# Chunk attention feeding a wave MLP: middle chunks' scores on four row tiles of TensorE, and another order of the whole program with q, k, v of the second group and q, k of the third loaded ahead of the token weights

## The chip, the cores and the metric

The kernel runs on one core of a Trainium2 chip. The core has five engines that each work through their own list of instructions: TensorE (PE in the profile; PEld is its weight load), VectorE (DVE), ScalarE (ACT), GpSimd (POOL) and SyncE (SP). DMAs are issued by POOL, SP and ACT and are carried by 16 DMA engines that all issuers share. The metric is the device time of one launch in microseconds; the median of the runs is what counts.

## The reference

Inputs are q, k, v of shape (8, 8, 576, 64) (batch, heads, sequence, head size) and four weight matrices. Attention works inside chunks of 64 positions:

```python
scores = scale * np.matmul(q_c, k_c.transpose(0, 1, 2, 4, 3))   # 9 chunks of 64 positions
scores = scores - np.max(scores, axis=-1, keepdims=True)
attn = np.exp(scores)
attn = attn / (np.sum(attn, axis=-1, keepdims=True) + 1e-09)
out = np.matmul(attn, v_c)
...
theta = x @ w_theta                                  # x: (8, 576, 512)
zr, zi = x * np.cos(theta), x * np.sin(theta)
y = np.einsum('ts,bsd->btd', w_tok_r, zr) + np.einsum('ts,bsd->btd', w_tok_i, zi)
u = x + y
return u + np.maximum(u @ w_ch, 0.0)
```

x is the attention output with the heads side by side. Everything is given and returned in float32; the kernel computes in float16 with float32 sums.

## The kernel before

**Tiles.** The batch is done in four pairs, p = 0 to 3. A pair's two sequences of 576 rows are nine tiles of 128 rows, j = 0 to 8: tiles 0 to 3 are the first four 128-row blocks of the first sequence, 4 to 7 those of the second, and tile 8 holds the last 64 rows of both, the "middle chunks". Attention goes by groups: A and B (tiles 0, 1 and 2, 3), C and D (4, 5 and 6, 7), each with four chunks of 64 positions, and M (tile 8) with two chunks, one of each sequence.

**Steps.** The program is a list of steps written out in one string, ORDER. A step "kind.where.slot" issues its instructions on its engines at that place; where is pair and group ("0M", "1A") or pair and tile ("37" is tile 7 of pair 3); the slot is a buffer or a PSUM bank (0 to 7). No scheduler moves anything afterwards, so each engine works in the order of the string. The kinds:

- qk, v: POOL issues the loads of a group's q and k (lines 158 to 175), or v (202 to 213), which cast to float16 on the way. q and k of an M group are four small DMAs, of any other group two; v is two or three. lw: token weights (242 to 247), lc: w_ch. hq, hk, lt: SP loads q, k of group 0A and w_theta as float32; cqa, ckv, cta cast them on ACT or DVE (196, 198, 262), ctv does it for w_theta on DVE.
- T (or Tq, Tk, Tk0, Tk1 for parts): DVE transposes q and k in 32x32 blocks (317).
- S (S0, S1: half of the heads): scores on PE (335), each product a 32-row by 64-column tile of the array. E: exponentials on ACT (361). V0, V1: times v on PE (378), N0, N1: division by the sum on DVE (393, 395).
- X: PE transposes x (415), xa and xv copy it to SBUF on ACT or DVE (440, 438); xd does both by one DMA transpose on SP's queue (432). H: theta on PE (453), G: cosine and sine on ACT (472), Z: x times them on DVE (488 to 495).
- TW: PE transposes a block of token weights (284), twv and twa copy it. Y (or Ya, Yb, Ym: parts of one sum): the token mix on PE (518), 18 products of 128x512 summed in one bank, or nine per half; A adds x on DVE (530).
- U with ua or uv: PE transposes u (535) and ACT or DVE copies it (547, 545); ud does it by a DMA transpose on SP's queue (543). W: times w_ch on PE (558), R: ReLU and sum on DVE (570); st, sa, sg: the store, issued by SP, ACT or POOL.
- dm.n.b: n products of a tile of zeros into bank b (154), which nothing reads.

**What sets the order of transfers.** POOL's loads go out in the order of the string, on eight semaphores in turn: a load isn't issued before the one eight places earlier has landed. In ORDER the first loads of POOL are q and k of 0M (four DMAs), v of 0M (two), v of 0A (three), token weights of block 2 (two), q and k of 0B (two), token weights 1 (two), v of 0B (three), token weights 0, q and k of 0C, token weights 3, and so on.

**Scores of an M group.** An M group has two chunks of 64 positions. Its q and k rows lie on partitions 0 to 63, a sequence on 32 of them (two positions in each), with all eight heads side by side, and after the transposes each product contracts over 32 partitions, twice (e = 0, 1). In the other groups the four chunks lie on the four quarters of 32 partitions, so that four row tiles of the array take turns; in an M group there are two. The innermost loop over c in lines 333 and 334 is this choice:

```python
for c in range(2 * n):                                  # n is 1 for an M group, else 2
    r, cc = (c // 2, c % 2) if n == 2 else (0, c)
    nc.tensor.matmul(ps[half[r ^ cc], r, h - hs[0]], ...)
```

r is the PSUM bank, half[...] the 64 partitions of it that are written.

Of the kernel before, what the change touches and what calls it, by code (L numbers as in the profile page):

```python
# [24 lines left out]
H0.0B.7 H1.0B.0 Tq.0C.0 G0.0B.2 G1.0B Tk.0C S.0C.3 twv.00 Ya.00.7 Z0.0B TW.03.5 Z1.0B Z.0M Yb.02  # L25
Ym.02 E.0C.3 Yb.00 Ym.00 A.02 Yb.01 Tq.0D.1 V1.0C.3 twa.03 A.00 V0.0C.0 Ym.01 Ya.03.5 Tk.0D
N1.0C S.0D.6 U.02.3 N0.0C ua.02.0 qk.1B.3 Yb.03 v.1M lw.04.2 X.0C.4 A.01 U.01.0 Ym.03 qk.1C.1
U.00.1 v.1B E.0D.0 A.03 V1.0D.2 N1.0D ua.01.1 qk.1D.4 qk.2M.12 v.1D V0.0D.6 xa.0C.3 v.2D qk.2C.5
v.1C W.02.0 N0.0D H.0C.4 U.03.2 ua.00.2 G.0C.0 T.1A.2 W.00.3 R.00.0 X.0D.1 S.1A.6 xv.0D.0 E.1A.1
v.2B qk.2A.6 W.01.3 H.0D.4 v.2M V0.1A.6 R.02.1 V1.1A.0 R.01.2 Ym.07.3 uv.03.3 G.0D.2 Ym.06.2  # L30
Z.0C N1.1A Ya.07 Ym.04.0 Ya.04 Ya.06 N0.1A W.03.1 X.1A.6 xa.1A.1 Z.0D Yb.06 T.1M.0 Yb.04 TW.04.4
R.03.3 twa.04 T.1B.1 S.1M.7 st.02 E.1M.2 A.04 A.06 S.1B.0 Yb.07 H.1A.4 V1.1M.6 qk.3M.7 qk.2B.8
v.2A A.07 N1.1M E.1B.3 V1.1B.2 st.01 V0.1B.0 N0.1B Y.08.7 V0.1M.6 N1.1B G.1A.1 U.06.0 ua.06.4
Ym.05.1 N0.1M X.1B.4 st.00 U.04.5 Ya.05 U.07.2 X.1M.3 xa.1B.2 A.08 T.1D.2 xv.1M.3 ua.04.5 H.1B.6
H.1M.0 v.3A qk.3A.9 ua.07.6 W.07.4 qk.3B.10 T.1C.0 G.1B.0 v.2C S.1C.2 S.1D.5 U.08.7 Yb.05 Z.1A
Z.1B G.1M.2 Z.1M uv.08.7 R.07.4 Y.12.0 E.1D.0 Y.11.7 v.3M A.12 E.1C.1 A.05 qk.3C.11 V0.1D.4
T.2M.1 V1.1D.2 V0.1C.0 Y.13.6 N1.1D W.08.2 N0.1D U.12.3 N0.1C A.11 X.1D.4 R.08.5 st.03 uv.12.0
T.2A.0 Y.10.5 A.10 A.13 V1.1C.0 S.2M.7 v.3C qk.2D.0 S.2A.2 N1.1C U.11.5 st.07 uv.11.2 W.06.6
st.08 X.1C.0 W.04.1 xa.1D.0 H.1D.4 E.2A.3 E.2M.2 R.04.1 R.06.3 U.05.2 xa.1C.1 T.2B.2 G.1D.1
H.1C.0 uv.05.1 T.2C.1 W.05.3 Z.1D st.04 R.05.2 S.2B.4 V1.2M.7 G.1C.0 Z.1C V0.2M.2 E.2B.0 sa.05  # L40
N1.2M W.11.6 U.10.0 ua.10.3 Y.17.1 N0.2M R.11.0 A.17 Y.15.7 V0.2B.4 V0.2A.2 A.15 N0.2B N0.2A
V1.2B.0 Y.18.6 A.18 S.2C.4 sa.11 X.2M.7 xv.2M.2 W.10.2 N1.2B R.10.4 E.2C.1 T.3M.0 H.2M.3 Y.16.6
U.13.7 G.2M.2 X.2B.4 V1.2A.0 A.16 st.06 st.10 uv.13.6 xa.2B.3 V0.2C.2 V1.2C.5 N1.2A N1.2C N0.2C
W.13.7 R.13.5 sa.13 X.2A.4 xd.2C.0 xv.2A.1 H.2B.0 U.18.5 U.17.6 U.16.2 uv.16.7 U.15.3 Y.14.7
ua.18.4 T.2D.2 Z.2M ua.17.5 ua.15.1 W.16.4 H.2A.5 G.2B.1 S.3M.2 S.2D.0 Z.2B G.2A.0 W.12.3 E.3M.2
R.16.1 A.14 Z.2A U.14.4 W.18.7 R.12.2 R.18.0 Y.21.5 Y.23.6 E.2D.0 st.18 V0.2D.2 T.3C.1 A.21
ua.14.2 v.3B T.3A.0 V1.2D.0 qk.3D.3 N1.2D N0.2D T.3B.2 sa.12 S.3A.4 W.14.7 sa.16 A.23 xd.2D.2
H.2C.0 E.3A.3 R.14.3 Y.22.4 G.2C.2 V0.3M.5 V1.3M.2 T.3D.0 A.22 Z.2C N1.3M st.14 S.3B.6 E.3B.1
S.3C.0 H.2D.3 E.3C.0 N0.3M W.15.6 Y.20.7 v.3D G.2D.1 ud.23.3 R.15.4 V0.3B.0 V0.3A.5 V1.3A.2 Z.2D
A.20 W.17.4 R.17.5 N0.3B Y.24.7 Y.27.4 N1.3A N0.3A A.27 V1.3B.0 xd.3M.3 N1.3B st.15 A.24 V1.3C.2  # L50
N1.3C S.3D.5 Y.28.4 H.3M.7 V0.3C.0 ud.20.6 E.3D.2 V0.3D.5 V1.3D.2 A.28 N0.3C N0.3D N1.3D xd.3A.1
G.3M.0 ud.27.7 W.27.4 Y.25.0 xd.3B.0 H.3A.5 A.25 ud.22.0 Y.26.1 G.3A.2 H.3B.2 ud.21.4 st.17 A.26
R.27.0 xd.3C.2 G.3B.1 H.3C.5 Z.3A W.21.7 xd.3D.3 Z.3M ud.24.2 G.3C.2 Z.3B R.21.2 Z.3C H.3D.0
# [11 lines left out]
def kernel(  # L65
# [11 lines left out]
    nc = tc.nc  # L77
# [226 lines left out]

    heads = {None: range(H), 0: range(H // 2), 1: range(H // 2, H)}

    def qk_t(which, f=None):

        def turn(p, g, slot=None):
            n = 64 if g == "M" else P  # L310
            if slot is not None:
                st["T", p, g] = buffer([P, 2, H, 32, 2, 2], "T", slot)
            a, z = {"q": (0, 1), "k": (1, 2), "qk": (0, 2)}[which]
            hs = slice(heads[f][0], heads[f][-1] + 1)
            src = st["qk", p, g][0:n, a:z, hs].rearrange("p w h s d -> p (w h s d)")
            to = st["T", p, g][0:n, a:z, hs].rearrange("p w h l s e -> p (w h l s e)")
            nc.vector.transpose(  # L317
                to.bitcast(FP32).rearrange("p (x l s) -> p x s l", l=32, s=2),
                src.bitcast(FP32).rearrange("p (x s d) -> p x s d", s=2, d=32),
            )  # L320

        return turn

    def scores(f):
        def products(p, g, b):
            n = size(g)
            hs = heads[f]
            ps = banks(b, n).rearrange("p (r x) -> p r x", r=n)[:, :, 0 : len(hs) * CH]
            ps = ps.rearrange("p r (h i) -> p r h i", i=CH)
            t = st["T", p, g].rearrange("p w h l s e -> p w h (l s) e")  # L330
            for h in hs:
                for e in range(2):
                    for c in range(2 * n):
                        r, cc = (c // 2, c % 2) if n == 2 else (0, c)
                        nc.tensor.matmul(  # L335
                            ps[half[r ^ cc], r, h - hs[0]],
                            t[quarter[c], 1, h, :, e],
                            t[quarter[c], 0, h, :, e],
                            start=(e == 0),
                            stop=(e == 1),  # L340
                            tile_position=(32 * c, CH * (r ^ cc)),
                        )
# [313 lines left out]
```

## Time and profile before

| | |
|---|---|
| runs | 194.37, 192.99, 193.19 us, median 193.19 |
| profiled execution | 194.09 us, its span 192.3 us |
| instructions in the profile | 6066, of them 2630 products on PE |

The span runs from the first to the last instruction of the core in the profile; 1.8 us of the profiled execution lie around it. All times below that are positions ("at 26.00") are microseconds from the start of the span. A line of a view in order of time gives start, length, engine, source line, operation and tile, how often, and in square brackets how long the engine had been idle and what ended that. A line of groups gives busy time, the mean of one instruction in nanoseconds, and the idle time ahead of them. The chain of waits follows the work that ended last back from the end, each piece with its start and length.

### The profile page before, as it was taken

What the parts mean: (1) busy time and instruction counts of PE and PEld (TensorE: products, weight loads), DVE (VectorE), ACT (ScalarE), POOL (GpSimd) and SP (SyncE); (2) the same over time, 40 slices, a digit from 0 to 9 for tenths busy, and PEclk for the clock granted to TensorE, in tenths of its full rate; (3) what the DMA queues carried; (4) which work ended last, traced back from release to release, by engine and by line L of the source; (5) the groups of instructions that cost most, each with busy time, mean ns of one, the idle gap of its engine ahead of it and who ended that gap; (6) DMA issues with size and microseconds to landing.
All of it is one profiled execution on the core that took longest, in us unless ns stands there. A gap on an engine that the chain in (4) does not pass through costs nothing.

```text
span 192.3 us, 6066 instructions
## 1 busy us (share of the span) xinstructions
PE 180.6 (94%) x2630; PEld 93.8 (49%) x2630; DVE 137.0 (71%) x254; ACT 101.2 (53%) x130; POOL 88.2 (46%) x125
## 2 busy tenths in 40 slices
PE   7569989999999999999999999999999999999980
PEld 2136445555464654555456554464544444444440
DVE  0155878967976988969788998967782963672761
ACT  3218797499759792289444665897164650000010
POOL 7788789579756996969388400000000000020400
PEclk9966999999999999999999999999999999999999
DMA  5999999999999999999999996542479217366693
GB/s 150 253 223 188 178 179 176 188 135 174 205 217 175 132 161 201 145 189 240 207 188 190 170 153 170 31 118 75 81 116 189 84 55 138 56 248 161 180 283 113
DMA packets 99002, 31.34 MB, mean 163 GB/s; under 512 B 90336, under 2 KB 94304, under 8 KB 98976
## 3 DMA queue, kind: packets, MB, share of 16 engines
q0 software_dynamic: 75568, 16.80, 95.2%
q1 hardware_dynamic: 21600, 11.01, 25.4%
q10 hardware_dynamic: 1808, 3.15, 4.5%
q8 instruction: 20, 0.33, 0.7%
q14 instruction: 6, 0.05, 0.1%
HBM read 33.06 MB, written 9.44 MB: 221 GB/s over the span
## 4 chain that ended last, share of the span: by engine, by line
PE 80%; DMA 6%; ACT 6%; DVE 3%; issue 1%; POOL 1%; DVEq 0%; POOLq 0%
PE psum L518 34%; PE psum L453 15%; PE psum L558 14%; PE psum L335 6%; DMA land<-in_k_dram 4%; PE psum L378 4%; DMA uT<-x 3%; PE psum L415 2%; PE psum L535 2%; ACT L140 2%; PE psum L154 2%; ACT cos L472 1%; ACT eT L361 1%; ACT sin L472 1%; PE psum L284 1%
## 5 line engine op out<-in xcount | busy, mean ns | idle before, releaser
L518 PEld LDWEIGHTS <-wT 128*128 128x128 f16 (+1 forms) x360 | 31.0, 100 | 34.5 <-issue 1.2
L210 POOL DMA_DIRECT2D v<-in_v_dram x56 | 41.9, 773 | 7.8 <-DMA land<-in_k_dram 2.7
L518 PE MATMUL psum<-zr,wT 128*128 128x512 f16 (+1 forms) x180 | 44.7, 380 | 0.0
L518 PE MATMUL psum<-zi,wT 128*128 128x512 f16 (+1 forms) x180 | 42.9, 379 | 0.0
L530 DVE TENSOR_TENSOR x<-psum,x 128x512 f16<-128x512 f32 x36 | 24.3, 685 | 19.4 <-PE psum L518 19.0
L558 PE MATMUL psum<-wch,uT 128*128 128x512 f16 (+1 forms) x148 | 35.4, 374 | 0.8 <-DMA uT<-x 0.8
L453 PE MATMUL psum<-wtheta,xT 128*128 128x512 f16 x144 | 34.2, 379 | 0.3 <-DVE xT L438 0.3
L586 POOL DMA_DIRECT2D out_dram<-o x4 | 2.2, 556 | 70.0 <-DVE o L570 70.0
L570 DVE SCALAR_TENSOR_TENSOR o<-psum,x 128x512 f32<-128x512 f32 (+1 forms) x37 | 24.0, 670 | 9.8 <-PE psum L558 9.7
L317 DVE STREAM_TRANSPOSE T<-land 128x1024 f32<-128x1024 f32 (+4 forms) x27 | 25.3, 949 | 8.0 <-DMA land<-in_q_dram 6.3
L361 ACT ACTIVATE eT<-psum 128x1024 f16<-128x1024 f32 (+1 forms) x22 | 18.2, 860 | 23.9 <-PE psum L335 21.6
L472 ACT ACTIVATE cos<-psum,pihalf 128x1024 f16<-128x1024 f32 (+1 forms) x22 | 21.1, 957 | 12.6 <-PE psum L453 11.5
L395 DVE TENSOR_TENSOR x<-psum,recip 128x512 f16<-128x512 f32 (+1 forms) x40 | 25.5, 638 | 1.4
L140 ACT ACT_TABLE_LOAD x20 | 25.7, 1283 | 1.1 <-PEq L640 0.7
L547 ACT COPY uT<-psum 128x512 f16<-128x512 f16 x12 | 6.8, 591 | 31.8 <-PE psum L535 31.8
L453 PEld LDWEIGHTS <-xT 128*128 128x128 f16 x144 | 13.5, 98 | 16.6 <-DVE xT L438 0.8
L558 PEld LDWEIGHTS <-uT 128*128 128x128 f16 x148 | 13.5, 98 | 14.9 <-DMA uT<-x 1.3
L472 ACT ACTIVATE sin<-psum 128x1024 f16<-128x1024 f32 (+1 forms) x22 | 19.0, 865 | 0.0
L335 PE MATMUL psum<-T 32*64 32x64 f16 x1152 | 14.4, 197 | 4.0 <-DVE T L317 4.0
L170 POOL DMA_DIRECT2D land<-in_q_dram x15 | 14.2, 946 | 7.6 <-DVE o L570 4.2
L335 PEld LDWEIGHTS <-T 32*64 32x64 f16 x1152 | 12.6, 109 | 8.5 <-DVE T L317 4.5
L170 POOL DMA_DIRECT2D land<-in_k_dram x15 | 13.6, 907 | 0.9 <-issue 0.5
(41 smaller groups left out, 143.2 us busy)
## 6 DMA issues: line engine op xcount, KB each, us to landing
out_dram<-o SPq DMA_DIRECT2D x16, 256.0 KB, 4.3
land<-in_q_dram POOLq DMA_DIRECT2D x15, 256.0 KB, 6.6
land<-in_k_dram POOLq DMA_DIRECT2D x15, 256.0 KB, 7.2
out_dram<-o ACTq DMA_DIRECT2D x11, 256.0 KB, 3.0
v<-in_v_dram POOLq DMA_DIRECT2D x40, 64.0 KB, 6.6
v<-in_v_dram POOLq DMA_DIRECT2D x16, 128.0 KB, 7.2
land<-in_moe_w_theta_dram SPq DMA_DIRECT2D x2, 512.0 KB, 7.0
out_dram<-o POOLq DMA_DIRECT2D x4, 256.0 KB, 2.9
```

Of the source, the lines that this page charges most:

```text
L140: nc.scalar.activation(out=first, in_=pihalf, func=func)
L170: nc.gpsimd.dma_start(t[:, w].rearrange("p h s d -> p h (s d)"), ap[2 * p + bb, :, s0 : s0 + GT, :].rearrange("h (p s) d -> p h (s d)", s=2),)
L210: nc.gpsimd.dma_start(v16[rows, slot + t, :, 0:D], v[b, :, t0 : t0 + m, :].rearrange("h s d -> s h d"),)
L317: nc.vector.transpose(to.bitcast(FP32).rearrange("p (x l s) -> p x s l", l=32, s=2), src.bitcast(FP32).rearrange("p (x s d) -> p x s d", s ...
L335: nc.tensor.matmul(ps[half[r ^ cc], r, h - hs[0]], t[quarter[c], 1, h, :, e], t[quarter[c], 0, h, :, e], start=(e == 0), stop=(e == 1), ti ...
L395: nc.vector.tensor_tensor(out=x.rearrange("p r (h d) -> p r h d", h=H // 2), in0=ps[:, :, :, 0:D], in1=recip[:, 0:n].broadcast_to((P, n, H ...
L453: nc.tensor.matmul(ps[:, (j - js[0]) * DM : (j - js[0] + 1) * DM], xT[:, j, a, :], wtheta16[:, a, :], start=(a == 0), stop=(a == NDB - 1),)
L472: nc.scalar.activation(out=t[:, js[0] : js[-1] + 1].rearrange("p j e -> p (j e)"), in_=ps, func=AF.Sin, bias=bias, scale=1.0,)
L518: nc.tensor.matmul(ps[half[c]] if j == MID else ps, wT[:, kt, t0 : min(t0 + P, S)], z, start=(b is not None and i == 0), stop=(i == len(kt ...
L530: nc.vector.tensor_tensor(out=x, in0=st.pop(("ps_y", p, j)), in1=x, op=ALU.add)
L558: nc.tensor.matmul(ps, uT[:, a, :], wch16[:, a, cols[f]], start=(a == 0), stop=(a == NDB - 1),)
L570: nc.vector.scalar_tensor_tensor(out=o, in0=ps, scalar=0.0, in1=st["x", p][:, j, cols[f]], op0=ALU.max, op1=ALU.add,)
```

## The change

Three things change; nothing else of the program differs.

1. **M groups keep half of their heads on the upper partitions.** The transposes (line 317 before) now take an M group in four pieces of 64 partitions by 256 instead of one of 64 by 1024 (q and k of 0M, which are turned apart, in two and two pieces instead of one and one): the source rows stay on partitions 0 to 63, and the results of heads 4 to 7 go to partitions 64 to 127. The scores loop takes four heads and four row tiles, so that an M group is still 32 products, on two banks instead of one. The exponentials read the two banks and write the same tile as before.

```diff
+    def heads_of(g):
+        return H // 2 if g == "M" else H
...
+            parts = [(slice(0, P), slice(a, z), hs, slice(0, P), hs)]
+            if g == "M":
+                parts = [
+                    (half[0], slice(w, w + 1), slice(n * i, n * i + n), half[i], slice(0, n))
+                    for w in range(a, z) for i in range(2)
+                ]
+            for rows, ws, hs, to_rows, to_hs in parts:
...
+                nc.vector.transpose(
...
-            n = size(g)
-            hs = heads[f]
-            ps = banks(b, n).rearrange("p (r x) -> p r x", r=n)[:, :, 0 : len(hs) * CH]
+            hs = heads[f][0 : heads_of(g)]
+            ps = banks(b, 2).rearrange("p (r x) -> p r x", r=2)[:, :, 0 : len(hs) * CH]
...
-                    for c in range(2 * n):
-                        r, cc = (c // 2, c % 2) if n == 2 else (0, c)
+                    for c in range(4):
+                        r, cc = c // 2, c % 2
+                        rows = cc if g == "M" else r ^ cc
                         nc.tensor.matmul(
-                            ps[half[r ^ cc], r, h - hs[0]],
+                            ps[half[rows], r, h - hs[0]],
```

2. **The order at the start.** ORDER begins

```diff
-pre.00 qk.0M.0 hq.0A.1 cqa.0A.2 hk.0A.3 Tq.0M.0 Tk.0M v.0M init.00 v.0A dm.21.7 S.0M.0 E.0M.0
-lw.02.4 qk.0B.5 dm.3.7 V1.0M.1 lw.01.6 v.0B ckv.0A lw.00.7 qk.0C.8 Tq.0A.1 Tk0.0A Tk1.0A dm.1.7
-S0.0A.2 S1.0A.4 E0.0A.1 lw.03.9 v.0C qk.0D.10 v.0D E1.0A lc.00 qk.1A.11 v.1A N1.0M dm.1.7
-V0.0A.6 N0.0A V0.0M.0 V1.0A.1 N1.0A dm.3.5 TW.02.3 lt.00.12 X0.0A.5 lt.01.1 twv.02 X1.0A.6
-xv0.0A.0 cta.01 xv1.0A cta.00 dm.2.7 H0.0A.7 Tq.0B.2 Tk0.0B Tk1.0B N0.0M H1.0A.1 S1.0B.2 G0.0A.0
-G1.0A Z0.0A dm.1.7 S0.0B.4 Z1.0A TW.01.6 X.0M.0 Ya.02.1 xv.0M.1 twv.01 E0.0B.2 V0.0B.4 N0.0B
-qk.1M.0 E1.0B V1.0B.6 N1.0B H.0M.0 Ya.01.2 X0.0B.3 X1.0B.4 TW.00.5 xv0.0B.2 G.0M.1 xa1.0B
+pre.00 hq.0A.0 hk.0A.1 cqa.0A.2 ckv.0A Tq.0A.0 lt.00.3 ctv.00 lt.01.4 qk.0M.5 v.0M
+init.00 Tk0.0A Tq.0M.1 qk.0B.6 v.0A Tk.0M dm.41.7 S.0M.0 S0.0A.2 Tk1.0A Tq.0B.2 E0.0A.0
+E.0M.1 Tk1.0B dm.5.7 V0.0M.4 V1.0M.5 N1.0M cta.01 S1.0A.6 dm.4.3 S1.0B.2 E1.0A Tk0.0B
+N0.0M dm.3.7 V1.0A.0 S0.0B.6 N1.0A v.0B V0.0A.4 qk.0C.7 X.0M.0 E0.0B.2 V0.0B.6 N0.0A
+E1.0B V1.0B.1 N1.0B N0.0B X1.0A.3 xa.0M.0 X0.0A.4 H.0M.5 xa0.0A.1 xv1.0A H0.0A.0 X0.0B.1
+X1.0B.2 G0.0A.0 xv0.0B.2 H1.0A.4 Tq.0C.1 H0.0B.6 xv1.0B lw.02.8 G1.0A lw.01.9 lw.00.10
+TW.02.0 H1.0B.7 Tk.0C Z1.0A twv.02 G0.0B.1 G1.0B Z0.0A G.0M.2 Z1.0B S.0C.2 qk.0D.11
+lw.03.12 Z0.0B TW.01.0 Ya.02.4 twa.01 TW.00.6 Z.0M Yb.02 Ym.02 twv.00 Ya.01.5 Yb.01
```

POOL's loads are now q, k and v of 0M (six DMAs), q and k of 0B (two), v of 0A (three), v of 0B (three), q and k of 0C (two), and only then the token weights of blocks 2, 1 and 0. SP's second load of w_theta has a buffer of its own and no longer waits for the cast of q. The zero products are 41 ahead of the first scores and 5 + 4 + 3 after them (before: 21, and 3 + 1 + 1 + 3 + 2 + 1).

3. **The order of the rest** is another one throughout, with the same steps, but some casts, copies and stores go to another engine or queue, and tile 7 of pair 3 (the last, "37") gets its u transposed by a DMA (ud.37) where PE and ACT did it (U.37, ua.37). A place in the middle, and the end from the last mix on:

```diff
+ua.06.5 uv.07.6 U.11.1 U.08.2 uv.08.7 X.1C.6 U.00.7 xv.1C.1 T.2B.0 H.1D.4 G.1D.2 H.1C.2
+G.1C.0 W.08.0 uv.11.0 T.2A.2 R.08.3 W.02.6 T.2C.1 sa.08 qk.2D.11 ua.00.1 U.12.1 Z.1C
+S.2B.4 E.2B.2 Z.1D S.2A.2 W.00.0 R.02.4 R.00.5 T.2M.0 sa.00 v.2B E.2A.3 ua.12.3 Y.10.7
...
-R.28.0 sg.28 Y.37.6 A.37 W.35.5 ud.31.7 ud.38.4 R.35.2 st.35 W.36.7 U.37.0 ua.37.2 R.36.3 sa.36
-W.31.3 R.31.5 st.31 W.22.1 W.38.4 R.22.4 sa.22 R.38.0 sx.38 W0.37.2 R0.37.2 st0.37 W1.37.0
-R1.37.3 sa1.37
+R.36.3 W.23.1 W.30.7 ud.24.7 W.27.0 sa.20 Y.37.2 R.30.5 R.27.4 ud.32.4 ud.35.5 R.23.2
+ud.38.2 ud.34.1 A.37 ud.31.6 sg.33 st.27 W.32.4 st.36 sg.23 W.38.6 R.38.0 sa.30 ud.37.3
+R.32.1 W.31.3 R.31.5 W.34.5 R.34.4 st.34 W.35.7 sa.38 W.28.0 sa.32 W.24.1 W1.37.2 R.35.3
+R.28.2 W0.37.6 st.31 R.24.0 R1.37.1 sg.35 sa.28 sa1.37 R0.37.4 sa0.37 st.24
```

More of the change, by code (lines that the diff above doesn't have):

```diff
@@ L24 @@
-qk.1M.0 E1.0B V1.0B.6 N1.0B H.0M.0 Ya.01.2 X0.0B.3 X1.0B.4 TW.00.5 xv0.0B.2 G.0M.1 xa1.0B
[L25 to L53, printed above, removed]
@@ L340, in products @@
                             stop=(e == 1),
-                            tile_position=(32 * c, CH * (r ^ cc)),
+                            tile_position=(32 * c, CH * rows),
                         )
@@ L354, in put @@
             table(AF.Exp)
-            if f is None:
+            if g == "M":
+                to = eT[:, :, 0].rearrange("p f h i -> p f (h i)")
+                ps = ps.rearrange("p f h i -> p f (h i)")
+            elif f is None:
                 to = eT[:, :, 0:n].rearrange("p f r h i -> p r f (h i)")
```

53 lines of the change are left out of this document (41 added, 12 removed).

## The prediction

> **What bounds the kernel now.** I read the page first, then a table of stretches, then the chain of waits in order of time, then the timelines of PE, DVE, POOL and SP at both ends.
>
> ```profile
> PE 180.6 (94%) x2630; PEld 93.8 (49%) x2630; DVE 137.0 (71%) x254; ACT 101.2 (53%) x130; POOL 88.2 (46%) x125
> ...
> PEclk9966999999999999999999999999999999999999
> ```
> ```profile
> 26.00:120.00 94.00, 94.00 (x1632) 51.83 (x1628) 79.51 (x143) 63.59 (x83) 63.78 (x85) 1.00 1.75 180
> 120.00:180.00 60.00, 59.79 (x669) 28.51 (x662) 39.95 (x72) 24.43 (x28) 1.68 (x3) 1.00 0.53 112
> ```
>
> The page gives busy time by engine and, in 40 slices, the clock granted to TensorE in tenths. The two rows below it are of the table of stretches: each has its length and the busy time of PE, PEld, DVE, ACT, POOL, then the granted clock, the DMA share and GB/s. From 26.00 to 180.00 PE is busy 153.8 of 154.0 us: there only less work on PE, or a new wait of PE, moves the end. The time that is not PE's lies in the first 26 us and in the last 12. In the first, PE also fills gaps with zero products. Its timeline shows what of use was done by 26.00:
>
> ```profile
> 1.20 6.02 PE L154 MATMUL psum<-zeros 128*128 128x512 f16 x21 [1.20 <-DVE pihalf L145]
> 11.26 1.06 PE L335 MATMUL psum<-T 32*64 32x64 f16 x32 [4.04 <-DVE T L317]
> ...
> 19.89 1.90 PE L453 MATMUL psum<-wtheta,xT 128*128 128x512 f16 x8 [0.27 <-DVE xT L438]
> ...
> 22.87 0.80 PE L284 MATMUL psum<-id,land 128*128 128x128 f16 x10
> ...
> ...
> 25.74 0.32 PE L378 MATMUL psum<-v,eT 64*64 64x65 f16 x16 [0.17 <-ACT eT L361]
> 26.00 1.04 PE L453 MATMUL psum<-wtheta,xT 128*128 128x512 f16 x4
> ```
>
> At 26.00 starts H.0M, and the last wait of any size is behind PE. H.0M is also the first theta of the changed order, so I use it as the mark: the new end is the new time of H.0M, plus what is left from there.
>
> **Part 1, the start.** The new PE order has, ahead of H.0M, the scores, the products with v and the transposes of x for 0M and 0A and the scores and products with v for 0B, as the old has; it lacks the two thetas of 0A (x8), two blocks of token weights (x10 each, the second is at 22.87) and Ya.02 (x4). What paces H.0M is the v of 0B, the fourteenth load of POOL. The fourteenth load before was a token weight, and each waits for the landing of the one eight earlier:
>
> ```profile
> 1.87 4.64 SPq L253 DMA_DIRECT2D land<-in_moe_w_theta_dram  x2
> ```
> ```profile
> 13.12 0.57 POOL L247 DMA_DIRECT2D land<-in_moe_w_tok_r_dram  x1
> ```
> ```profile
> land<-in_moe_w_theta_dram SPq DMA_DIRECT2D x2, 512.0 KB, 7.0
> ...
> land<-in_moe_w_tok_r_dram POOLq DMA_DIRECT2D x4, 144.0 KB, 6.3
> ```
> ```profile
> 11.13 0.64 DVE L198 CAST land<-land 128x1024 f16<-128x1024 f32 x1
> ```
> ```profile
> L317 DVE STREAM_TRANSPOSE T<-land 128x256 f32<-128x256 f32 x4 | 1.4, 398 | 0.0
> ```
>
> Issued at 13.12 and 6.3 under way, it landed at about 19.4. The first fourteen loads held 1584 KB before (M 384, v of 0A 256, three token loads of 144, q and k 512) and hold 1408 KB now (M 384, q and k 512, twice v 256); at 180 GB/s (the stretch from 26 to 120) the difference is 1.0 us, of which I take half: 19.0. Then follow two products with v (0.32 each) and two times four transposes of x (0.22 each, below: eight in 0.45), so H.0M starts at 20.0: 6.0 earlier. Ends: 19.2 and 21.5 (the second load of w_theta no longer waits and crowds POOL's loads). Of 6.0, the work that is still to be done goes off, priced in the chain, where a piece ends as the next starts:
>
> ```profile
> 28.34 0.62 PE psum L284 x10
> 28.97 1.83 PE psum L453 x8
> 30.80 0.64 PE psum L335 x64
> 31.44 0.97 PE psum L518 x4
> ...
> 44.10 0.86 PE psum L558 x4
> 44.96 0.45 PE psum L415 x8
> ...
> 55.99 1.16 PE psum L335 x84
> ```
>
> 1.83 + 2 x 0.62 + 0.97 = 4.0. The start gains 2.0.
>
> The first scores come later: DVE now has the cast of w_theta ahead of the transposes of 0M. w_theta's first half is issued at 1.87 on SP and takes 7.0, so 8.9, or up to 9.6 with the second beside it, which I take; the cast 0.64, Tk0 0.40, four pieces of 64x256. No row shows these; 128x256 takes 0.40, and half the partitions may cost half; I take 0.40, as the columns are the same. That makes 12.2, against 11.26. It costs nothing while v of 0B is due at 19; if that cover were gone, 0.9. The 41 zero products end at about 11.8 (21 took 6.02, and 20 more of that shape at full clock, as theta's 1.83 for eight, 0.23 each). So PE has no idle stretch of 4.04 us there as before, which was followed by two slices of clock 0.6. I take the full clock for the new start; the other case is a rival.
>
> **Part 2, scores of M.** The piece at 55.99 holds an M group (32 products) and one of 64 (some records are missing); 1.16 - 0.64 leaves 0.52 for 32 on two row tiles. At the rate of four, 64 in 0.64, 32 take 0.32: 0.2 less, for the three M groups behind the mark 0.6. The ends are 0 and 0.8. [...] DVE's four pieces (4 x 0.40 = 1.6 per group, in all) lie on an engine 71% busy, at places where PE has token mixes queued: nothing.
>
> **Part 3, the rest of the order.** U.37 goes (0.22, four transposes; it becomes a DMA). I looked for places where a step is now close behind what feeds it, and found two. The first: W.00 needs ua.00, which stands on ACT behind G.1D, G.1C and the two stores sa.08.
>
> ```profile
> 43.92 1.11 ACT L472 ACTIVATE cos<-psum,pihalf 128x1024 f16<-128x1024 f32 x1
> 44.93 1.02 ACT L472 ACTIVATE sin<-psum 128x1024 f16<-128x1024 f32 x1
> ```
> ```profile
> 169.75 1.53 ACTq L586 DMA_DIRECT2D out_dram<-o  x3
> 183.29 0.59 ACT L547 COPY uT<-psum 128x512 f16<-128x512 f16 x1 [25.84 <-PE psum L535]
> ```
>
> From the end of H.1D ACT needs 2 x (1.11 + 1.02) + 2 x 0.51 + 0.59 = 5.9 (three stores took 1.53 to issue); PE has H.1C 1.83, W.08 and W.02 0.86 each, U.12 0.22 and two scores of 0.64, 5.0. A wait of 0.9, and behind W.00 stands everything of PE. Ends: 0, and 2.1 more if another cosine and sine are late.
>
> The second is the last stage:
>
> ```profile
> L543 SPq DMA_TRANSPOSE uT<-x x17: 1189/1222/1481, 124.9 to 180.9; - x17
> ```
> ```profile
> uT<-x SPq DMA_TRANSPOSE x17, 2.7
> ```
> ```profile
> 180.86 4.86 DMA uT<-x
> ```
> ```profile
> 185.76 1.91 PE L558 MATMUL psum<-wch,uT 128*128 128x512 f16 x12 [0.78 <-DMA uT<-x]
> ```
> ```profile
> GB/s 172 129 222 76 0 0 0 0 77 211 15 369 250 215 80 352 266 206 112 148 243 127 223 426 393 412 365 379 284 24 14 66 213 294 294 322 24 0 0 0
> ```
>
> W.31 is the third W behind Y.37, and its u comes as the fifth of five transposes in a row on SP (1.22 each to issue, 2.7 to land by the median). If it lands as late as the one at 180.86, 2.2 over the median, PE waits some of that; I take 1.0, ends 0 and 2.2. The wait of before, 0.78 ahead of 185.76, goes with its step.
>
> PE's last product ended at 187.7. Now: 187.7 - 6.0 + 4.0 - 0.6 - 0.2 + 0.9 + 1.0 - 0.8 = 186.0.
>
> From there to the end of the span at 192.3 it was 4.6 (last ReLU, store, landing). Behind Y.37 stand 13 stores of 256 KB now, 6 before. The row of GB/s (40 slices from 175 to 192.3) reaches 426, and 290 over the slices of the last stores: 0.62 to 0.90 each, so 13 take 8.1 to 11.7. Y.37 starts at 186.0 - 8 W x 0.86 - 1.0 - 1.94 (twice the 0.97 of half a mix) = 176.2, and the first goes out some 0.5 later: all have moved by 184.8 or by 188.4. What follows the move was 4.6 less about 0.5 for the ReLU and 0.6 for the move, 3.5: at the worst the span ends at 191.9, against 186.0 + 4.6 = 190.6 if the stores don't limit. I take 191.1, nearer to PE's end, since several queues share the fast rate. That is 1.2 under the span of 192.3, so 192.9 for a profiled execution (before 194.09), and 192.0 against the median of 193.19, which is 0.9 under that execution.
>
> **Rivals.** A measurement of this kernel can tell about 1% from no change: faster is below 191.26, slower above 195.12.
>
> - The two new waits don't come (ACT runs ahead, the transposes are issued before PE gets there): 1.9 less, 190.1. For it: ACT is busy 53%, and SP has nothing else to do. Against: in the order the pairs stand as close as counted. Chance 0.18.
> - Slower: the last transposes. ud.37 is issued as the sixth on SP, behind two stores; the trace shows 4.86 for a transpose while stores ran, and now 13 stores run. The last W halves are due at 176.2 + 1.94 + 7 x 0.86 = 184.2, a wait of 1.0 ahead of them left out. A.37 needs Y.37's end at 178.1 and some 0.7, so a ud.37 that lands over 5.4 after A.37 decides: with an issue held to 181 and 4.9 to land, 185.9, and W.31 2.2 late, all of it goes on the end, with the stores behind it at 0.90: +3.4 to 195.4. Chance 0.17.
> - PE's clock falls to half at the start in spite of the zero products. Between 11.8 and 17.8 PE has some 4 us of work at full clock; of the doubling, about half is hidden by waits for v: +1.9, 193.9. Chance 0.08. [...]
> - The start doesn't do what it says: with w_theta whole on SP's queue, POOL's loads come late, H.0M at 21.5 or later, and the scores gain nothing: +1.5 + 0.6, 194.1. Chance 0.12.
>
> **How the numbers follow.** The forecast, 192.0, has 0.45; its own range is 190.7 to 193.3 (the stores 0.6 less or 1.3 more), and a third of it lies under 191.26. Faster is 0.18 + 0.15 = 0.33. Slower is 0.17. Same is the rest, 0.50. The range leaves out about one in ten at each side: 190.0 to 195.0.
>
> **What would show each step.** H.0M on PE's timeline at about 20, with a clock of 1.0 in the slices from 10 to 19; v of 0B as what PE waited for just ahead. The scores of an M group as 32 in about 0.3. A wait of about 1 us of PE for ACT's uT near the fifth tenth of the span, and one for a DMA uT in the last 12 us. The stretch from H.0M to 180 otherwise without idle PE. Wrong would be: PE waits in the middle that I didn't count, an end that is set by a DMA and not by PE's last product, or a half clock at the start.

## The result, and the profile after

The changed kernel takes 195.41 us (median of 9 runs, 194.09 to 195.87), the kernel before, measured beside it, 193.22 (9 runs, 192.11 to 194.51): ratio 1.0108, interval 1.0079 to 1.0136. That is about 1% slower, outside the range of 190.0 to 195.0. The profiled execution took 194.92, with a span of 192.9.

The page of the changed kernel, busy time by engine and the clock granted in 40 slices:

```profile
PE 183.4 (95%) x2647; PEld 95.3 (49%) x2647; DVE 139.0 (72%) x264; ACT 93.0 (48%) x118; POOL 88.3 (46%) x126
...
PEclk9999699999999999999999999999999999999997
```

PE is about as busy as it was; the row of the clock has a dip in its fifth slice (19.3 to 24.1), where none was expected. The table of stretches (length, busy time of PE, PEld, DVE, ACT, POOL, clock, DMA share, GB/s), cut at the start of H.0M:

```profile
0.00:22.47 22.47, 19.47 (x306) 9.94 (x306) 9.79 (x25) 6.71 (x10) 16.99 (x29) 0.93 1.48 199
22.47:120.00 97.53, 97.27 (x1607) 53.53 (x1605) 82.56 (x160) 63.47 (x82) 67.44 (x90) 1.00 1.63 162
120.00:180.00 60.00, 59.47 (x704) 28.56 (x703) 40.55 (x71) 22.81 (x26) 3.03 (x6) 1.00 0.58 131
```

Behind H.0M PE stands for 0.8 us in 157.5 (0.2 in the 154 of before). What happened ahead of it is on PE's timeline:

```profile
12.40 0.80 PE L354 MATMUL psum<-T 32*64 32x64 f16 x64
...
17.25 0.32 PE L400 MATMUL psum<-v,eT 64*64 64x65 f16 x16
17.50 0.28 PE L354 MATMUL psum<-T 32*64 32x64 f16 x10
19.57 0.53 PE L354 MATMUL psum<-T 32*64 32x64 f16 x22 [1.78 <-issue]
20.03 0.44 PE L400 MATMUL psum<-v,eT 64*64 64x65 f16 x16
20.40 0.61 PE L437 MATMUL psum<-id,x 128*128 128x128 f16 x4
20.93 0.77 PE L400 MATMUL psum<-v,eT 64*64 64x65 f16 x32
21.64 1.04 PE L437 MATMUL psum<-id,x 128*128 128x128 f16 x8
22.47 2.08 PE L475 MATMUL psum<-wtheta,xT 128*128 128x512 f16 x8
```

The second scores of 0B (S0.0B, 32 products) break after the tenth; PE stands 1.78 us, and "issue" says that it waited for nothing that the profile shows. Behind the stand everything is slow: four transposes took 0.61, and 0.40 in a later trace at full clock. The table of stretches by the microsecond gives the clock:

```profile
18.00:19.00 1.00, 0.00 (x0) 0.00 (x0) 0.63 (x1) 0.00 (x0) 0.53 (x1) 1.00 1.96 178
19.00:20.00 1.00, 0.43 (x22) 0.39 (x21) 0.00 (x0) 0.00 (x0) 0.00 (x0) 0.72 1.87 180
20.00:21.00 1.00, 1.00 (x30) 0.70 (x28) 0.45 (x2) 0.86 (x2) 0.87 (x2) 0.50 1.55 197
21.00:22.00 1.00, 1.00 (x37) 0.89 (x37) 0.62 (x2) 0.70 (x2) 1.00 (x2) 0.50 1.24 201
22.00:23.00 1.00, 1.00 (x9) 0.72 (x7) 0.93 (x4) 0.29 (x1) 0.46 (x2) 0.58 1.21 203
```

Finer stretches put the half clock from 19.4 to 22.85, 3.4 us. The loads were later than forecast as well. On POOL's timeline, where the three loads of v of 0B are issued from 11.73 on, the first load of token weights 0 waits for the load eight places earlier, the second part of v of 0B, which therefore landed at 20.1, where 19.0 was forecast for v of 0B:

```profile
11.73 2.25 POOL L213 DMA_DIRECT2D v<-in_v_dram  x3 [1.18 <-DMA land<-in_k_dram]
...
20.13 0.53 POOL L250 DMA_DIRECT2D land<-in_moe_w_tok_r_dram  x1 [1.38 <-DMA v<-in_v_dram]
```

The list of PE's waits (total, times, longest) holds the rest:

```profile
PE psum L354 <- issue: 1.8, 1, 1.8
...
PE psum L580 <- DMA uT<-x: 0.7, 1, 0.7
PE psum L475 <- DMA xT<-x: 0.5, 1, 0.5
PE psum L580 <- ACT uT L569: 0.3, 1, 0.3
```

The last three are the wait in the last stage (forecast 1.0), one that was not forecast (H.2C, whose x is turned by a DMA), and W.00's for ua.00 (forecast 0.9). The scores of M did become shorter. The same 96 products (an M group of 32 and a group of 64) on PE's timeline, first of before, then of after:

```profile
55.92 1.23 PE L335 MATMUL psum<-T 32*64 32x64 f16 x96
```
```profile
54.22 0.98 PE L354 MATMUL psum<-T 32*64 32x64 f16 x96
```

0.25 us less per M group. The last products of PE, on its timeline, and the last stores of SP and ACT (the q after the engine's name marks its DMA queue):

```profile
182.43 5.36 PE L580 MATMUL psum<-wch,uT 128*128 128x512 f16 x28 [0.65 <-DMA uT<-x]
```
```profile
186.82 1.13 ACTq L605 DMA_DIRECT2D out_dram<-o  x2
...
187.68 0.33 SPq L608 DMA_DIRECT2D out_dram<-o  x1
188.05 1.41 ACTq L608 DMA_DIRECT2D out_dram<-o  x2
```

PE ends at 182.43 + 5.36 = 187.79, the span 5.1 later. The sum of the forecast beside this trace:

| | forecast | measured |
|---|---|---|
| H.0M starts | 20.0 | 22.5 |
| from there to PE's last product | 166.0 | 165.3 |
| from there to the end of the span | 5.1 | 5.1 |
| around the span | 1.8 | 2.0 |
| from the profiled execution to the median | -0.9 | +0.5 |
| time | 192.0 | 195.4 |

Two rows hold the miss: the start (2.5) and the last step (1.4); the stretch between gave back 0.7.

### The profile page after: what moved, and what is told of

Its sections match the earlier page's. It is cut to its first block, busy times and chain, and to the rows that moved or that the text cites. A ratio compares the mean times of both kernels' runs of the same rounds, so it can differ in the third digit from the quotient of the medians.

```text
span 192.9 us, 6099 instructions
## 1 busy us (share of the span) xinstructions
PE 183.4 (95%) x2647; PEld 95.3 (49%) x2647; DVE 139.0 (72%) x264; ACT 93.0 (48%) x118; POOL 88.3 (46%) x126
## 4 chain that ended last, share of the span: by engine, by line
PE 88%; DMA 4%; issue 2%; ACT 2%; DVE 0%; ACTq 0%; DVEq 0%
PE psum L540 37%; PE psum L475 15%; PE psum L580 14%; PE psum L157 7%; PE psum L354 5%; PE psum L400 4%; PE psum L437 3%; DMA xT<-x 2%; PE psum L557 2%; DMA uT<-x 2%; PE psum L287 2%; ACT sin L494 1%; ACT cos L494 1%; ACTq L605 0%; ACT uT L569 0%
## 5 line engine op out<-in xcount | busy, mean ns | idle before, releaser
L608 POOL DMA_DIRECT2D out_dram<-o x7 | 3.8, 549 | 76.7 <-DVE o L592 76.7
L580 PE MATMUL psum<-wch,uT 128*128 128x512 f16 (+1 forms) x148 | 34.9, 374 | 0.9 <-DMA uT<-x 0.7
L335 DVE STREAM_TRANSPOSE T<-land 64x256 f32<-64x256 f32 (+3 forms) x38 | 27.5, 729 | 1.6 <-DMA land<-in_k_dram 0.8
L494 ACT ACTIVATE cos<-psum,pihalf 128x1024 f16<-128x1024 f32 (+1 forms) x22 | 21.1, 961 | 11.7 <-PE psum L475 11.0
L173 POOL DMA_DIRECT2D land<-in_q_dram x15 | 13.6, 906 | 4.9 <-DMA land<-in_k_dram 2.4
L157 PE MATMUL psum<-zeros 128*128 128x512 f16 x53 | 14.4, 431 | 1.2 <-DVE pihalf L148 1.2
L354 PE MATMUL psum<-T 32*64 32x64 f16 x1152 | 13.5, 194 | 1.8 <-issue 1.8
L462 ACT COPY xT<-psum 128x1024 f16<-128x1024 f16 (+1 forms) x8 | 7.3, 906 | 15.2 <-PE psum L437 9.7
```

The lines of the kernel that those rows point to most:

```text
L157: nc.tensor.matmul(banks(b), zeros[:, 0:P], zeros)
L173: nc.gpsimd.dma_start(t[:, w].rearrange("p h s d -> p h (s d)"), ap[2 * p + bb, :, s0 : s0 + GT, :].rearrange("h (p s) d -> p h (s d)", s=2),)
L335: nc.vector.transpose(to.bitcast(FP32).rearrange("p (x l s) -> p x s l", l=32, s=2), src.bitcast(FP32).rearrange("p (x s d) -> p x s d", s ...
L354: nc.tensor.matmul(ps[half[rows], r, h - hs[0]], t[quarter[c], 1, h, :, e], t[quarter[c], 0, h, :, e], start=(e == 0), stop=(e == 1), tile ...
L494: nc.scalar.activation(out=t[:, js[0] : js[-1] + 1].rearrange("p j e -> p (j e)"), in_=ps, func=AF.Sin, bias=bias, scale=1.0,)
L580: nc.tensor.matmul(ps, uT[:, a, :], wch16[:, a, cols[f]], start=(a == 0), stop=(a == NDB - 1),)
```

## The experiments

Each ratio is to the kernel before, measured beside it on the same chip. The groups of kernels measured together went to different chips, and the changed kernel differed more between them than the kernel before did (195.3 and 196.1, against 193.2 and 192.6), so versions of it are compared within a group where that can be.

**Part 1 alone, and part 1 taken out.** First the M groups' scores on four row tiles, in the old order, with the moves that the second bank forces:

```diff
-S.1M.7 ... V1.1C.0 S.2M.7 v.3C qk.2D.0 S.2A.2 ... W.12.3
+S.1M.6 ... V1.1C.0 S.2M.6 v.3C qk.2D.0 S.2A.2 E.2M.2 ... W.12.6
```

> The kernel before with part 1 alone: the M groups' scores on four row tiles and their transposes in four pieces, in the old order (for the second bank, S.1M, S.2M and W.12 take other banks, E.2M stands a few steps earlier and A.13 ahead of A.10). Scores theory: in the trace of the changed kernel 96 score products take 0.98 us where 96 took 1.23, so 0.25 us less per M group; three of the four groups lie where PE is never idle: 0.75 us less, ratio 0.996, about 192.4. Rival, the four DVE pieces delay a later transpose that PE waits for: no gain or a loss, ratio 1.000 to 1.005, and a new wait of PE for DVE's T in its list of waits.

Measured: 194.24, ratio 1.0045 (1.0009 to 1.0081), about half a per cent slower. Its list of PE's waits has what the list of before has not:

```profile
PE psum L575 <- ACT sin L489: 1.2, 1, 1.2
PE psum L349 <- DVE x L547: 1.1, 2, 0.7
```

W.12 now waits for the bank that G.2A frees (1.2), and scores wait twice for DVE (1.1). Scores that want two banks don't fit into this order as it was made for one; 0.75 us gained on PE stands against 2.3 us of new waits in this trace (of the slowest of the twelve executions). The second kernel has the changed order with the old scores, and the transposes and exponentials that belong to them:

```diff
-                    for c in range(4):
+                    for c in range(2 * n):
```

> The changed order with the scores of the M groups on two row tiles as before (part 1 undone, nothing else). Scores theory: 0.75 us slower than the changed kernel's 195.4, so about 196.2, ratio 1.015 to the kernel before. Rival, the gain of the scores is hidden by waits elsewhere in the new order: 195.4, ratio 1.011. If part 1 is itself what costs: below 195, ratio under 1.008.

Measured: 194.90, ratio 1.0101 (1.0050 to 1.0151). So part 1 isn't most of what made the changed kernel slower. Its gain can't be seen in the time either, but an interval of 1 us to each side can't rule out the 0.75 us. Its trace has the stand in the scores of 0B too (1.54 us, at the same product), but full clock behind it, and H.0M at 21.57.

**Splices of the two orders.** The old start with the changed rest, and the changed order up to 125 us with the old rest:

```diff
-(changed order up to X1.0A, H.0M)
+(old order up to and with H.0M) X0.0B.4 X1.0B.2 xv0.0B.2 ...
```

> The old order up to and with H.0M, then the changed order's remaining steps (X0.0B takes another bank), scores of M on four row tiles. Start theory: the changed start brings H.0M to only 22.5 us and leaves 4.0 us more work behind it, so the old start is better by 0.5 us by the two traces and by as much as 2 if the start also varies more; with it this kernel comes out at 193.4 to 194.9, and nearer 193.4 if all of the loss is in the start; ratio 1.001 to 1.009. Rest theory (the loss is in the middle or the last stage): within 0.5 us of 195.4, ratio 1.009 to 1.013.

```diff
-(changed order behind R.10)
+v.3C st.10 sa.13 U.15.3 ua.15.1 W.16.4 (old order's remaining steps)
```

> The changed order up to R.10 (about 125 us), then the old order's remaining steps, so the old last stage with U.37 on PE and six stores behind Y.37 instead of thirteen; one uT tile has a buffer of its own. Tail theory (thirteen stores and the late transposes cost): the tail from PE's last product to the end goes from 5.1 to about 4.6 us and the wait ahead of the last W products goes: 193.2 to 194.2, ratio 1.000 to 1.005. Start theory: the loss stays, 195.0 to 195.6, ratio 1.009 to 1.012.

Measured: 196.09 (1.0130, 1.0089 to 1.0170) and 198.91 (1.0274, 1.0221 to 1.0327). Neither tells what it was meant to: the first trace shows 1.5 us of new waits of PE within 6 us behind the cut, the second 3.5 us in four waits between 129 and 138. The first also has a stand of 1.05 us in the scores of 1A, at 41.8, that ends by "issue" like the one of the changed kernel: such a stand isn't bound to the changed start. A step taken out of the order that feeds it waits, whichever order it is put into. A cleaner cut came later, at 40 us:

```diff
-dm.21.7 ... A.00 (old order)
+dm.41.7 ... A.00 Ym.01 Tk.0D S.0D.0 A.01 V0.0C.5 (changed order's remaining steps, sa0.37 as st0.37)
```

> The old order, with 41 zero products ahead of the first scores, up to and with A.00 (about 40 us); behind it the changed order's remaining steps, with M's scores on four row tiles and the last half store on SP; S.0D takes another bank. A cleaner cut than the first splice, whose trace showed 1.5 us of new waits of PE right behind the cut. Start theory (the loss is in the changed start, 1.5 to 2.5 us; the changed rest is no worse than the old but for 0.5 us at the end): 192.0 to 193.0, ratio 0.993 to 0.999, PE's last product 160.5 to 161.5 us behind the start of H.0M. Rest theory: 194.0 or more, ratio 1.004 or more.

Measured: 195.92 (1.0187, 1.0134 to 1.0240), which the start theory doesn't give. Its trace has no stand at the start and no half clock, H.0M at 24.78, PE's last product at 188.26, so 163.5 behind it. But it has a wait at the cut again:

```profile
41.29 0.71 PE L349 MATMUL psum<-T 32*64 32x64 f16 x64 [1.61 <-DVE T L330]
```

Without that wait 161.9 would be left, where 160.5 to 161.5 was expected and the old order has 161.5 to 162.1 in four traces (three of them described below). I read from this only that the changed rest has no advantage over the old one that reaches the end.

**A second trace of the changed kernel.**

> The changed kernel once more, for a second trace. If the idle 1.78 us of PE inside the scores of 0B (17.78 to 19.57, ended by nothing that the profile shows) belongs to the program, it is there again, after the same tenth product; if it was an accident, it is gone and H.0M starts near 21.0 instead of 22.5. Half clock behind it (0.50 from 19.6 to 22.6 in the first trace, 1.00 in the trace of the changed order with the old scores) may or may not come. Time 195.0 to 195.8, ratio 1.008 to 1.013.

Measured: 195.26, ratio 1.0096 (1.0058 to 1.0133). The stand is there again, at the same product, with half clock behind it (0.50 at 20 to 22) and H.0M at 22.20:

```profile
19.30 0.53 PE L354 MATMUL psum<-T 32*64 32x64 f16 x22 [1.71 <-issue]
```

It belongs to the program. At 41.32 its timeline shows a second one, of 0.20, in S.1A.

**Is the place fixed in PE's list?** Ten zero products fewer ahead of it:

```diff
-dm.41.7
+dm.31.7
```

> The changed kernel with 31 zero products ahead of the first scores instead of 41. [...] Accident theory, or a wait for data that the profile misses: the break stays after the tenth product or is gone. PE stands 2 to 3 us ahead of the first scores; the time of a single run tells nothing here.

PE's timeline of this kernel:

```profile
17.41 0.35 PE L349 MATMUL psum<-T 32*64 32x64 f16 x20
19.84 0.29 PE L349 MATMUL psum<-T 32*64 32x64 f16 x12 [2.07 <-issue]
```

The break moved from the tenth product to the twentieth, so it keeps its place in PE's list of instructions; a wait for data would have kept its product. It doesn't keep its time: with the late splice and with fewer stores (below) these scores came some 0.5 us later, and the break, at 18.35 and 18.24 instead of 17.78, still followed the tenth product. (196.74 in one run, of which nothing is concluded.) In the stretch from 16 to 19 of the changed kernel's trace the table of DMA queues (packets, MB, share of 16 engines) has one packet of a queue that it names "instruction":

```profile
q8 instruction: 1, 0.02, 2.5%
```

The traces without a stand have such a packet there too (2.0% in the first trace of the kernel before, 2.4% in the next experiment), so the row doesn't tell them apart. What PE stood for is not shown by any view. From 12.40 to 17.78 PE goes through 182 products, all but 12 of them short. The kernel before has nearly as many in its start (172 from 11.26 to 19.61), but behind them come eight long ones, the theta of 0A.

**Long products in that place.** The transposes and theta of 0M move ahead of S0.0B:

```diff
-N0.0M dm.3.7 V1.0A.0 S0.0B.6 N1.0A v.0B V0.0A.4 qk.0C.7 X.0M.0 E0.0B.2 V0.0B.6 N0.0A
-E1.0B V1.0B.1 N1.0B N0.0B X1.0A.3 xa.0M.0 X0.0A.4 H.0M.5 xa0.0A.1
+N0.0M X.0M.4 xa.0M.0 E1.0B.2 dm.3.7 V1.0A.0 H.0M.5 S0.0B.6 N1.0A v.0B V0.0A.2 qk.0C.7
+E0.0B V0.0B.6 N0.0A V1.0B.0 N1.0B N0.0B X1.0A.3 X0.0A.4 xa0.0A.1
```

> The changed kernel with the x transposes and theta of 0M (eight products with 1 us of work) put ahead of the second scores of 0B, and the second exponential of 0B ahead of its first; V0.0A, V1.0B, X.0M and E1.0B take other slots. [...] Rest theory (the loss is behind H.0M): 0.0 to 0.4 us less, ratio 1.007 to 1.012.

Measured: 194.50 (1.0068, 1.0033 to 1.0104), 0.76 less than the changed kernel beside it (195.26), where the rest theory has 0.4 at the most, but the two intervals overlap. PE's timeline:

```profile
18.46 1.04 PE L470 MATMUL psum<-wtheta,xT 128*128 128x512 f16 x4
19.43 0.45 PE L349 MATMUL psum<-T 32*64 32x64 f16 x32
...
22.54 1.04 PE L470 MATMUL psum<-wtheta,xT 128*128 128x512 f16 x4 [0.68 <-ACT xT L457]
```

The scores are whole, the clock is 1.00 up to 180 us, and the first theta of 0A stands at 22.54, where the changed kernel's first trace has it at about 23.4 (22.47 and four products) and its third, with full clock, at about 22.7.

**What of it is the clock?** Where a trace showed half clock in the start, it lasted 3.4 us (19.4 to 22.85 in the changed kernel's first) or 6.8 (10.7 to 17.5 in the first of the kernel before). In the nine traces with the changed start and no long products in that place, H.0M stands at 22.2 to 23.5 in the five with such a stretch behind the stand, and at 21.3 to 21.8 in the four without. Their stands differ too (1.3 to 2.4 us); in the first and third traces of the changed kernel the stand ends at the same 19.57, and H.0M comes at 22.47 with half clock and 21.84 without. By this pair half clock costs the start some 0.6 us, and without it H.0M is still late.

How many executions have it is less sure, as those without a trace have only a mean clock. Of 22 executions of the changed kernel 13 had a mean under 0.99; their spans were 193.8 in the mean, those of the other nine 192.7. This sorts only roughly: the second trace, with half clock at the start, has 0.991, and half clock behind PE's last product (0.50 from 191 on in the changed kernel's first trace) counts as well. In the kernel before, 11 of 24 executions measured together were under 0.99 and took no longer (191.5 against 191.4 in the mean). Of the 16 executions of the two versions with long products there (the second follows below) two were under 0.99, and the mean of the others is 192.5.

The zero products of the changed start in the kernel before, whose trace also had half clock:

```diff
-dm.21.7
+dm.41.7
```

> The kernel before with 41 zero products ahead of the first scores instead of 21, nothing else: this one piece of the changed start alone. Clock theory (the idle 4.04 us of PE ahead of the first scores lets the clock fall to 0.50 from 10.7 to 17.5 in the trace, and that costs): no slice under 0.9 in the first 20 us and H.0M earlier than 26.0 by 0.5 to 1.9 us: ratio 0.990 to 0.997. Rival, the start is paced by loads and the slow clock is hidden by the waits for them: H.0M within 0.3 us of 26.0 and a ratio of 0.998 to 1.002. A loss is possible if the zero products end later than the first transposes: 41 took 11.3 us in the changed kernel, to 12.4, where the first scores stood at 11.26: then up to 1.1 us later, ratio up to 1.006.

Measured: 193.31, ratio 1.0028 (0.9996 to 1.0060). The trace (192.09 for its execution) has full clock and H.0M at 24.18, as the clock theory wants it, but the time is not better, as the rival wants it. Both can be true if the first trace of the kernel before, with H.0M at 26.0, shows an execution that is not its usual one. Two more traces of it:

> The kernel before once more, for a second trace. Its first trace had the clock at 0.50 from 10.7 to 17.5, H.0M at 26.0 and a span of 192.3, while the median span of its other executions is 191.5; with 41 zero products instead of 21 H.0M stood at 24.2. If the first trace was an unlucky execution: H.0M at 24.5 to 25.5 here, span near 191.5, and the changed start (H.0M at 21.3 to 22.5 with 3.5 us more left) is later by 0 to 1.5 us. If it was the usual one: H.0M at 25.7 to 26.2 again with half clock, and the changed start costs nothing by itself.

> The kernel before, a third trace, for the same question: H.0M at 24.5 to 25.5 if the first trace was an unlucky execution, 25.7 to 26.2 if it was the usual one. From PE's last product to the end of the span 4.5 to 4.7 in either case.

Measured: spans 190.3 and 190.8, H.0M at 23.84 and 24.13, though the clock falls in both (0.57 and 0.75 at 11 to 13, 0.57 and 0.50 at 13 to 15). PE's timeline of the first of these two, and the table of stretches with its clock:

```profile
10.30 0.69 PE L335 MATMUL psum<-T 32*64 32x64 f16 x32 [2.80 <-DVE T L317]
...
23.84 1.04 PE L453 MATMUL psum<-wtheta,xT 128*128 128x512 f16 x4
```
```profile
11.00:13.00 2.00, 2.00 (x20) 0.64 (x24) 1.59 (x5) 0.60 (x1) 2.00 (x3) 0.57 2.18 175
13.00:15.00 2.00, 2.00 (x105) 1.49 (x105) 0.21 (x2) 1.41 (x3) 1.92 (x4) 0.57 1.43 191
```

So the old start can be 2 us better than in the trace on which the forecast stood, with half clock too. The late start is no single accident either: part 1 alone and the first splice have the same start, and their H.0M stands at 25.90 and 24.59. The clock sorts these five traces: it was at half for 6.8 us where H.0M stands at 26.0 and 25.9, and for 3.4 us where it stands at 23.8, 24.1 and 24.6 (the first scores come 0.2 to 1.0 us later in the two late ones, so the clock need not be all of it). Against this trace, the third one of the changed kernel (below), with full clock, has H.0M 2.0 earlier (21.84), 3.5 more to PE's last product (165.4 against 161.9), and 0.5 more behind it (5.1 against 4.6): 2.0 in all, the difference of the spans (192.3 and 190.3).

**The end.** Six stores left out (tiles 20, 23, 30, 32, 33, 38):

```diff
-sg.33 ... sg.23 ... sa.20 ... sa.30 ... sa.38 ... sa.32
```

> The changed kernel without six of its last stores (tiles 20, 23, 30, 32, 33 and 38 of the result aren't stored; all six were issued by POOL and ACT, so the order on SP is as it was). Tail theory (thirteen stores behind Y.37 are moved by a saturated queue): from PE's last product to the end of the span 4.5 us or less instead of 5.1, and uT of the last tiles lands earlier, so PE's wait of 0.65 ahead of the last seven W goes: together 0.8 to 1.5 us less than the changed kernel, ratio 1.000 to 1.005. Rival, the last store alone sets the end by its own latency: no change, 195.0 to 195.8, ratio 1.008 to 1.013.

Measured: 195.20 (1.0093, 1.0054 to 1.0132), no gain, and 5.6 us from PE's last product to the end: the tail theory falls in this form, though PE's wait for uT is gone. (The stand at the start was 2.4 us in this trace.) Then the last half store on SP:

```diff
-sa0.37 st.24
+st0.37 st.24
```

> The changed kernel with the very last half store (tile 37, the half that is ready last) issued by SP instead of ACT, nothing else. Issue theory: in the trace of the changed kernel ACT issues that store at 188.69, 0.64 behind the one ahead of it on the same queue, and the old kernel had the two halves on two queues (188.16 and 188.22); with SP it goes out at about 188.1, and the span ends 0.5 us nearer to PE's last product: 4.5 to 4.7 us behind it instead of 5.1, ratio about 1.007. Queue theory (all stores share the 16 engines, and the last lands when the bytes are through): 5.0 or more, ratio 1.009 to 1.011.

Measured: 195.87 (1.0179, 1.0126 to 1.0232), on a chip without the changed kernel beside it; the trace has 5.5 us behind PE's last product. The edit only made another store the last: the full store st.24 now waited on SP behind the half store. Third, the three full stores nearest to the end left out (tiles 35, 24, 28), with the changed kernel beside it:

```diff
-sg.35 sa.28 ... st.24
```

> The changed kernel without the three full stores that are issued in its last 2.5 us ahead of the last half stores (tiles 35, 24 and 28 of the result aren't stored); the six earlier ones that the run with fewer stores left out are back. End theory (the last half stores wait behind bytes issued just ahead of them): from PE's last product to the end of the span 4.6 us or less instead of 5.1 to 5.6, the last store lands within 2.9 us of its issue instead of 3.2, ratio about 0.003 under that of the changed kernel in the same call. Rival, it is the issue on ACT and a fixed latency: 5.0 us or more, no change in time.

> The changed kernel, for the comparison on this chip and for a third trace: 194.9 to 195.9, PE standing 1.3 to 2.4 us after the tenth product of the second scores of 0B, H.0M at 21.3 (full clock there) to 22.5 (half clock behind the stand).

Measured: 194.54 (1.0090, 1.0053 to 1.0128) and 196.05 (1.0173, 1.0119 to 1.0227). PE's last products of the shortened kernel, on its timeline:

```profile
181.79 5.36 PE L574 MATMUL psum<-wch,uT 128*128 128x512 f16 x28 [0.82 <-DMA uT<-x]
```

187.15, and its span ends at 191.4: 4.25 behind, against 5.1 in the changed kernel. This is what the end theory expects. Leaving out tile 28 also freed ACT, which has issued its last half store 1.05 us behind PE's last product here and 1.67 in the changed kernel, so this run alone doesn't tell bytes from issue; the next one does. Both edits that gained or seemed to, in one kernel:

```diff
-st.31 R.24.0 R1.37.1 sg.35 sa.28 sa1.37 R0.37.4 sa0.37 st.24
+st.31 R.24.0 st.24 R1.37.1 sg.35 sa.28 sa1.37 R0.37.4 st0.37
```

> The version with the theta of 0M ahead of the second scores of 0B, and at the end the full store of tile 24 issued by SP ahead of the half store that is ready last, which is now SP's last (ACT has the other half): what the runs so far point to. Sum of the parts: start 0.6 to 0.9 less than the changed kernel, end up to 0.5 less: ratio to the changed kernel 0.993 to 0.996, about 194.0, still 0.5 us or more over the kernel before, as v of 0B lands no earlier. If start and end were not what costs: as the changed kernel.

Measured: 194.40 (1.0108, 1.0058 to 1.0158), 1.65 less than the changed kernel in its six runs beside it; the two intervals overlap a little. The mean clock of the execution is 1.000. In the scores of 0B a short break is left:

```profile
18.82 0.22 PE L349 MATMUL psum<-T 32*64 32x64 f16 x2
19.30 0.44 PE L349 MATMUL psum<-T 32*64 32x64 f16 x30 [0.27 <-issue]
```

It follows the second product, and eight products of 0M were moved ahead of these scores: ten less eight, the same place in PE's list. The last half store has been issued 1.07 us behind PE's last product, as early as in the kernel without the three stores, but the span ends 5.3 behind that product instead of 4.25. The last half store took 3.6 us to land, against 2.4 in the median of the two halves there, though on another queue (SP, not ACT). So what the three stores cost is, for most of it, the time to land and not the time to issue; issuing them in another order gave nothing. PE's last product comes 0.3 earlier than in the changed kernel's third trace, which has full clock at the start; the rest of the 1.65 isn't seen in a trace, and that it is the clock is not shown. No version beat the kernel before.

## Why the prediction was wrong

**The step that failed** is part 1, "so H.0M starts at 20.0": it started at 21.8 to 22.5 in three traces, past the end of 21.5 that I gave it. Three terms make up the 2.5 of the first trace. The v of 0B landed at 20.1, not 19.0 (1.1; its third part came by 20.65, when the load eight places behind it went out without a wait, so this term may be larger and the next one smaller). It was issued about when I thought, but I gave it the 6.3 us under way of a token weight; its second part, issued at 12.6, took 7.5. The page of the kernel before had slower loads of v on it already:

```profile
v<-in_v_dram POOLq DMA_DIRECT2D x40, 64.0 KB, 6.6
v<-in_v_dram POOLq DMA_DIRECT2D x16, 128.0 KB, 7.2
```

Then PE stood 1.7 to 1.8 us in the scores of 0B, which no row of the kernel before shows: with S0.0B late, ACT began its exponential at 20.1 and the products with v went at 20.9 (0.8). From there to H.0M it took 1.5 us where 1.0 was counted (0.5): the third trace, at full clock, has 1.2, as the second exponential comes behind the first, and half clock makes the rest. Against an H.0M at 24 in the old order, one at 22 is 2 us earlier, with the 4.0 of work left behind that I had counted: the start loses 2 where a gain of 2 was forecast. (The two traces compared above have 3.5 instead of 4.0, with the gain of the scores of M and the waits of the rest in it.)

**The rival that I gave 0.12** (H.0M at 21.5 or later) is the one that came, but in part for other reasons: the scores of M did gain. The first loads of POOL were crowded: k of 0M, issued as before, landed at 11.7, where it had landed by 10.8. Whether w_theta did it, or q and k of 0B, which also go out earlier now, no run separates, and the issue of v of 0B was no later than forecast. That of half clock, at 0.08, came too, in the first two of three traces, not between 11.8 and 17.8 but behind the stand. Its low chance was an estimate of mine that was worked out from no run: in the first trace PE had stood 1.78 us, with the 182 products ahead of it, and the clock went to 0.50; in the third it had stood 1.84, and the clock stayed at 1.00.

**The base** failed as well. I measured the start against a trace with H.0M at 26.0 and took 0.9 off at the end for the median. Two more traces have H.0M 2.2 and 1.9 earlier, and spans 2.0 and 1.5 shorter: what the first was over them lay in just the stretch that the change replaces, and the 0.9 could not be carried over to the changed kernel. The last step of the sum was 1.4 off. 0.9 of that is this; the other 0.5 is that the changed kernel's profiled execution happened to be faster than its median. Against an H.0M at 24, even the forecast 20.0 would only have paid for the 4.0 of work left behind.

**What held.** From H.0M to PE's last product 166.0 was forecast and 165.3 measured. The scores of M gained 0.25 per group (1.23 to 0.98 for the 96 products) where 0.2 was taken. W.00 waited 0.3 or less for ACT, not 0.9, and the last stage 0.65 to 0.84 for uT, not 1.0; the 0.5 for H.2C's x was missing. The 5.1 us behind PE's last product came out to the tenth, but that was luck, as my reason (13 stores behind Y.37) is not the one: five of them and one ahead fewer changed nothing, the last three fewer did.

**The slower rival**, ud.37 landing late, didn't come: in the changed kernel's first trace W0.37 is in a run of 28 products without a gap.

## What to carry to other kernels

Take more than one trace of the kernel before when the change replaces a stretch that varies: here two executions of it (spans of 192.3 and 190.3) differed by as much as the change was worth. Starting a stage earlier is worth its time only less the work that is pushed behind it. The start that was packed with short products had PE standing 1.3 to 2.4 us at a place of its list where nothing that the profile shows was missing; with 1 us of long products moved there, 0.27 us or nothing was left of the stand. A gain on a full engine (here 0.25 us per M group) shows in the time only if the waits around it (2.3 us of new ones in the old order) don't take it back.

## What the runs showed of the hardware

- PE stood 1.3 to 2.4 us at one place of its list, after 182 mostly short products in 5.4 us; the place moved by ten products when ten fewer stood ahead and by eight when eight more did, and with 1 us of long products there the stand was 0.27 us in one trace and absent in another.
- Half clock at the start lasted 3.4 us in six traces by their tables of stretches, and 6.8 us in two; in those of the two splices the mean clock up to 170 us was 0.99, which 3.4 us of it gives. It came behind a stand of 1.78 us, and not behind one of 1.84 in another execution of the same program.
- In the kernel before, an idle time of 2.80 us ahead of the first scores was followed by 3.4 us of half clock between 11 and 15 us, and H.0M came 2 us earlier than in the trace with 4.04 us idle and 6.8 us of half clock.
- The span ended 4.25 us behind PE's last product without three full stores in the last 2.5 us, and 5.3 us with them, though the last half store had been issued as early (1.05 and 1.07 us behind that product).
